# Two seams of a fused attention, gated MLP and expert kernel: splits queued behind the last unit, a check moved, rooms dealt anew

## The chip, the cores and the metric

The kernel runs on one core of a Trainium2 chip. The core has five engines with a queue each: TensorE (PE, matrix products, with its weight loads as PEld), VectorE (DVE), ScalarE (ACT), GpSimd (POOL) and SyncE (SP, which issues most transfers). The metric is the device time of one execution in microseconds. Three executions of the kernel before took 591.48, 587.75 and 591.14 us: the median is 591.14.

## The reference, cut to what matters

Three stages follow one another. B = 2 batches, S = 576 tokens, H = 8 heads of 64, width 512.

```python
# 1. attention in which each row keeps its 32 largest scores
scores = q @ k.T / 8
kth = the 32nd largest score of each row
attn = softmax(where(scores >= kth, scores, -1e9))
x = concatenated heads of attn @ v                        # (2, 576, 512)
# 2. gated MLP that mixes along the tokens
h = gelu(x @ w_in)                                        # 1024 wide
u, v = halves of h
v_n = layernorm(v) * g_ln
v_s = einsum('ts,bsd->btd', w_sg, v_n) + b_sg             # the spatial product
x = x + (u * v_s) @ w_out
# 3. mixture of 8 experts, one per token
logits = x @ w_gate
fresh = argmax(logits)
# a token takes its own choice when it is the first or sigmoid(x @ w_local) < 0.5, else its predecessor's
out = p[e] * (relu(x @ w1[e]) @ w2[e])
```

## The kernel before

**Units.** The attention is cut into tiles of 128 queries and these into units, one head of one tile each: 36 in each batch, 72 in all (`unit`, L348). A unit makes its scores on TensorE (L289), copies them (ScalarE, L292), finds a threshold from maxima (VectorE L318 to L335, ScalarE L329, GpSimd L333), takes exponentials (L331), and masks them: every second unit on VectorE (L345), the others with a sign on ScalarE (L342) and a product on GpSimd (L343). TensorE transposes the result (L357), ScalarE copies it as `pt` (L360), and TensorE multiplies it by the values (L365, `pv`). When four units are through, VectorE divides by the sums and writes the rows (L370 to L382). There is one `pv` buffer, so the next four wait for that.

**Steps between units.** A list `between` holds steps of the later stages, and `pump` (L736) takes some after each unit: the input product of the MLP for a finished tile (`mlp_in`), then, after the last unit, `tail` (L680). `tail` is the spatial product of batch 0 and of batch 1 (`spread`), and `finish`, which works out the logits and the route and projects (`project`, L594) each tile with `w_out`, adds `x` (L610) and writes the rows to `xrows` in device memory (L612). The list `written` keeps these ten writes; the last two belong to the tile that holds the end of both batches.

**Splits.** The products of `spread`, `logits` and `project` work on numbers split in two parts: `in_two` (L453) copies the upper part on ScalarE (L455) and subtracts it on VectorE or GpSimd (L456). `parts` (L480) splits the spatial weights (ScalarE and GpSimd) and the activations of batch 0 (ScalarE and VectorE), five bands each, with one band more of the weights for the second batch; `parts_late` those of batch 1, `parts_out` the projection's weights. The parts lie in rooms of earlier tiles that are no longer in use (`of_scores`, `of_weights`, `of_rest`, `of_queries`, `of_values`).

**The check.** After `attention`, L1081 to L1097 look whether the fast search for the threshold held in every unit, and put a flag in `fi`. The program reads it after the experts; if it is set, everything is done again with an exact search.

**The experts.** `experts` (L817) opens pools of its own in the same memory. VectorE sorts the experts by their counts (L830 on), gives each token a slot (`split`, L854), and a product (`in_slots`, L874) turns slots into token numbers. GpSimd gathers the rows of `xrows` by these numbers, 128 slots at a time (L907); `take` (L934) transposes them into `xw`. SyncE reads the experts' numbers into registers (L1009) and loads the weights (`load_expert`, L952), the first half of the first expert's `w1` behind the last write of `xrows`, the rest behind the second gather. `expert` (L969) makes both products, `give` (L941) writes the result. `KEEP` products without use (L998) stand between the projection and the experts, and `WARM` such products (L802) at the start.

**What sets the order.** Each engine works its queue in order. The orders are made at build time by a planner that simulates the engines with modelled costs: at each step an engine takes, of the instructions that are ready, the one of highest priority. That is its place in the program, moved ahead by `tc.high_priority(offset=...)` (AHEAD for the units, EVAC for the copies out of the accumulators). So an instruction that is ready early may be placed long before its place in the program. `tc.issue_after(ins)` orders what is issued within it behind `ins` on the engine of `ins`, and on no other. A tile whose room is still in use waits for the release.

Of the kernel before, what the change touches and what calls it, by code (L numbers as in the profile page):

```python
# [11 lines left out]
F32 = mybir.dt.float32  # L12
# [15 lines left out]
AHEAD = 2000  # L28
# [9 lines left out]
WARM = 14  # L38
KEEP = 30
# [3 lines left out]
def tile_topk_gmlp_moe(  # L43
# [123 lines left out]
    def attention(fast):  # L167
# [115 lines left out]

        def scores(b, j, i):
# [27 lines left out]
        def weights_fast(s_sb, un):  # L312
# [24 lines left out]
            if MASK[un % len(MASK)] == "a":  # L337
# [5 lines left out]
                nc.gpsimd.tensor_tensor(e_sb, e_sb, mask, op=OP.mult)  # L343
# [4 lines left out]
        def unit(b, j, i, fast):  # L348
# [10 lines left out]
            pt = wk.tile([P, NJ, P], F32, name="pt", bufs=2)  # L359
            nc.scalar.activation(pt.rearrange("p t q -> p (t q)"), pt_ps[:, :NJ * P], AF.Relu)  # L360
# [6 lines left out]
            if i % g == g - 1:  # L367
# [9 lines left out]
                for a in range(w):  # L377
# [3 lines left out]
                    nc.vector.tensor_tensor(xo[to, :, a, :], pv[r, :, a, :D],  # L381
                                            rc[r, :, a, None].to_broadcast([n, g, D]), op=OP.mult)  # L382
# [97 lines left out]
        def parts():  # L480
# [5 lines left out]
            rooms = [of_scores, of_scores] + [of_weights] * 5 + [of_queries] * 3  # L486
# [12 lines left out]
        def parts_late():  # L499

            sg = wts.tile([P, NJ, S], F32, name="w_sg_sb").bitcast(F32R)
            rooms = of_values(F2) + [sg[:, j, :F2] for j in range(NJ)]
# [4 lines left out]
            rooms += [kv.tile([P, S], F32, name="kk", bufs=6).bitcast(F32R)[:, :F2] for _ in range(6)]  # L507
            for f in range(CF):
                UT2[1, f] = (rooms.pop(0), rooms.pop(0))

        def parts_out():
            rooms = [of_weights] * 5 + [of_queries] * 3
            for f in range(CF):
                OUT2.append((rooms.pop(0)(), rooms.pop(0)()))
# [12 lines left out]
        def spread(b):  # L527
# [3 lines left out]
            def step(f, n, j):  # L531
# [3 lines left out]
                if j == js[0] and f == 0 and n == 0:  # L535
                    (parts, parts_late)[b]()
# [603 lines left out]
```

## Time and profile before

| | |
|---|---|
| median of 3 runs | 591.14 us (587.75 to 591.48) |
| the profiled execution | 589.88 us, of which its span 588.1 us |
| TensorE busy | 519.8 us, 88% of the span |
| VectorE, ScalarE, GpSimd busy | 349.1, 307.8, 260.4 us |
| mean granted clock of TensorE | 0.972 |
| transfers | 61.57 MB, mean 105 GB/s |

The span runs from the first to the last instruction of the profiled execution, and all times inside it count from its start. The attention with the input products fills the time to about 345 us, the spatial product and the projection that to about 413 us, the experts the rest. The granted clock is a mean over a stretch: 1.00 is 2.4 GHz, 0.50 is 1.2 GHz. In brackets, a row of a timeline gives the idle time of the engine before it and what ended that.

### The profile page before, as it was taken

The page shows a single profiled execution, that of the slowest core. Times are in us where ns is not written, and L with a number is a line of the kernel's source. Part 1 is how long each engine was busy: PE and PEld are TensorE (multiplying, and loading weights), DVE is VectorE, ACT ScalarE, POOL GpSimd, SP SyncE. Part 2 cuts the span into 40 slices and gives each one's busy share as a digit, 9 for nine tenths or more (in the row PEclk, how much of TensorE's full clock was granted, in tenths as well). Part 3 has the DMA queues.
Part 4 walks back from the last instruction along what each step waited for, and adds up shares of the span by engine and source line. Part 5 has one row for each costly group of instructions (what it writes and reads, how often), then busy time and mean ns, then how long its engine had stood idle before and what let it go on. Part 6 is the DMA issues. An engine that isn't in the chain of part 4 may idle for free. (4 is left out here: it accounts for less than half of the span.)

```text
span 588.1 us, 10456 instructions
## 1 busy us (share of the span) xinstructions
PE 519.8 (88%) x3477; PEld 450.8 (77%) x3478; DVE 349.1 (59%) x1643; ACT 307.8 (52%) x566; POOL 260.4 (44%) x382
## 2 busy tenths in 40 slices
PE   6568698998989898999967899999699999999992
PEld 3447576867778787878857788968399999999992
DVE  4798998989798999999982335764201111111110
ACT  3579879898799989889881614210020111011110
POOL 6497796777667676785855121010220101000010
PEclk9799999999999999999997999999989999999996
DMA  8953210002000002110000000014599997684000
GB/s 175 259 155 111 100 45 6 25 2 75 12 28 20 16 13 82 48 35 17 7 7 20 16 3 1 1 58 150 175 337 386 388 386 269 232 297 162 18 36 17
DMA packets 42610, 61.57 MB, mean 105 GB/s; under 512 B 14056, under 2 KB 18152, under 8 KB 42544
## 3 DMA queue, kind: packets, MB, share of 16 engines
q1 hardware_dynamic: 40880, 55.80, 28.9%
q0 software_dynamic: 1664, 4.97, 2.5%
q8 instruction: 31, 0.51, 0.4%
q14 instruction: 35, 0.29, 0.2%
HBM read 53.68 MB, written 7.33 MB: 104 GB/s over the span
## 5 line engine op out<-in xcount | busy, mean ns | idle before, releaser
L365 PE MATMUL pv<-v,pt 128*128 128x128 f32 (+1 forms) x720 | 101.6, 280 | 8.5 <-DVE row L381 7.1
L333 POOL TENSOR_TENSOR rest<-s_sb,sg 128x576 f32<-128x576 f32 x72 | 93.7, 1302 | 30.5 <-ACT sg L329 29.5
L289 PE MATMUL s_ps<-kk,q 128*128 128x288 f32 x288 | 86.7, 424 | 21.1 <-ACT s_sb L292 20.2
L365 PEld LDWEIGHTS pv<-v,pt 128*128 128x128 f32 x720 | 94.1, 195 | 13.8 <-issue 6.3
L318 DVE MAX8 cand<-s_sb 128x8 f32<-128x72 f32 x576 | 90.0, 222 | 9.2 <-ACT s_sb L292 9.0
L289 PEld LDWEIGHTS s_ps<-kk,q 128*128 128x128 f32 x288 | 50.3, 194 | 37.3 <-ACT s_sb L292 26.8
L357 PE MATMUL pt_ps<-ident,e_sb 128*128 128x128 f32 x360 | 65.1, 281 | 15.5 <-ACT pt L360 8.5
L976 PE MATMUL h_ps<-xw,w_sb 128*128 128x152 f32 (+6 forms) x512 | 78.2, 302 | 0.0
L987 PE MATMUL y_ps<-hT,w_sb 128*128 128x152 f32 (+6 forms) x512 | 75.3, 299 | 0.0
L976 PEld LDWEIGHTS h_ps<-xw,w_sb 128*128 128x128 f32 x512 | 72.9, 192 | 0.4
L987 PEld LDWEIGHTS y_ps<-hT,w_sb 128*128 128x128 f32 x512 | 71.1, 190 | 0.0
L979 ACT ACTIVATE hT<-h_ps 128x152 f32<-128x152 f32 (+6 forms) x32 | 9.7, 302 | 113.9 <-PE h_ps L976 113.1
L357 PEld LDWEIGHTS pt_ps<-ident,e_sb 128*128 128x128 f32 x360 | 44.4, 145 | 27.7 <-issue 6.3
L329 ACT ACTIVATE sg<-s_sb,last 128x576 bf16<-128x576 f32 x72 | 55.6, 772 | 10.8 <-DVE last L321 7.1
L360 ACT ACTIVATE pt<-pt_ps 128x640 f32<-128x640 f32 x72 | 50.3, 698 | 17.0 <-PE pt_ps L357 16.1
L335 DVE MAX8 next<-rest 128x8 f32<-128x583 f32 x72 | 54.8, 761 | 6.4 <-POOL rest L334 6.1
L331 ACT ACTIVATE e_sb<-s_sb,nm 128x576 f32<-128x576 f32 x72 | 55.7, 774 | 4.2 <-POOL nm L326 2.1
L948 POOL DMA_INDIRECT out_dram<-orow,to x10 | 10.0, 1001 | 103.1 <-ACT orow L947 48.3
L292 ACT ACTIVATE s_sb<-s_ps 128x576 f32<-128x576 f32 x72 | 46.4, 644 | 17.0 <-PE s_ps L289 15.1
L343 POOL TENSOR_TENSOR e_sb<-e_sb,mask 128x576 f32<-128x576 f32 x36 | 46.2, 1282 | 16.6 <-ACT mask L342 7.8
L981 DVE TENSOR_SCALAR hT<-h_ps 128x152 f32<-128x152 f32 (+6 forms) x32 | 10.3, 323 | 71.9 <-PE h_ps L976 66.5
L989 DVE COPY yT<-y_ps 128x152 f32<-128x152 f32 (+6 forms) x32 | 9.9, 323 | 64.6 <-PE y_ps L987 64.6
(285 smaller groups left out, 871.7 us busy)
## 6 DMA issues: line engine op xcount, KB each, us to landing
w_sb<-in_w_dram SPq DMA_DIRECT2D x32, 1024.0 KB, 10.5
dbl<-in_w_in_dram SPq DMA_DIRECT2D x8, 512.0 KB, 4.6
kk<-in_kT_dram SPq DMA_DIRECT2D x8, 288.0 KB, 4.2
q<-in_qT_dram SPq DMA_DIRECT2D x32, 64.0 KB, 2.3
v<-in_v_dram SPq DMA_DIRECT2D x8, 256.0 KB, 6.1
dbl<-in_w_out_dram SPq DMA_DIRECT2D x4, 512.0 KB, 3.8
xin<-row SPq DMA_DIRECT2D x8, 256.0 KB, 2.0
back<-xin SPq DMA_DIRECT2D x8, 256.0 KB, 2.8
```

The costliest lines, as they stand in the source:

```text
L289: nc.tensor.matmul(s_ps[:, n, :HS], QH[b, j, h], KK[b, pair][:, n * HS:(n + 1) * HS], start=True, stop=True)
L292: EVACS.append(nc.scalar.activation(s_sb.rearrange("p (n s) -> p n s", n=2), s_ps[:, :, :HS], AF.Copy))
L318: nc.vector.max(cand[:, 8 * g:8 * g + 8], s_sb[:, g * w:(g + 1) * w])
L329: nc.scalar.activation(sg, s_sb, AF.Sign, bias=last8[:, un, 7:8], scale=-LESS, accum_out=cnt)
L331: nc.scalar.activation(e_sb, s_sb, AF.Exp, bias=nm, scale=scale)
L333: nc.gpsimd.tensor_tensor(below[:, :S], s_sb, sg, op=OP.mult)
L335: nc.vector.max(next8[:, un, :], below)
L357: tr = nc.tensor.transpose(pt_ps[:, t * P:(t + 1) * P], p_sb[:, k0:k0 + P], ident)
L360: nc.scalar.activation(pt.rearrange("p t q -> p (t q)"), pt_ps[:, :NJ * P], AF.Relu)
L365: nc.tensor.matmul(PV[b][:, i % g, :], pt[:, t, :], V1[b][:, t, w * i * (D + 1):w * i * (D + 1) + nv], start=t == 0, stop=t == NJ - 1)
L976: nc.tensor.matmul(hp[:, :W], w1_sb[:, c, f * P:(f + 1) * P], xw[:, c, at], start=c == 0, stop=c == CD - 1)
L987: nc.tensor.matmul(yp[:, :W], w2_sb[:, f, c * P:(c + 1) * P], hT[:, f, :W], start=f == 0, stop=f == CE - 1)
```

## The change

It does eight things:

- `WARM` goes from 14 to 7, `KEEP` from 30 to 24; the `KEEP` products are queued behind the first product of the search for slots.
- The last mask product on GpSimd, the last `pt` copy on ScalarE and the last row write on VectorE are noted in `ENDS`, and `parts` and `parts_late` are issued behind them, each engine behind its own.
- The rooms of the split parts change. The parts of the gated `u` go from `w_in` to rooms of the values, `w_sg` and the keys; the batch-1 activations to rooms of the raw loads and of `xT`; the projection's weights to the room of `w_in`.
- `logits` takes its small buffer from `of_rest`.
- In `experts`, `xw` and the gathered rows get pools that are opened ahead of the search's pool `rt`, and `w2` is laid out ahead of `w1`. So the search's tiles lie elsewhere.
- The search has twice the priority offset.
- The first half of the first expert's `w1` is issued behind the fourth last write of `xrows`; the second half stays behind the last.
- The check becomes a function and is called after the second expert.

```diff
-WARM = 14
-KEEP = 30
+WARM = 7
+KEEP = 24
...
+        ENDS = {}
...
-                nc.gpsimd.tensor_tensor(e_sb, e_sb, mask, op=OP.mult)
+                ENDS["g"] = nc.gpsimd.tensor_tensor(e_sb, e_sb, mask, op=OP.mult)
...
-            nc.scalar.activation(pt.rearrange("p t q -> p (t q)"), pt_ps[:, :NJ * P], AF.Relu)
+            ENDS["a"] = nc.scalar.activation(pt.rearrange("p t q -> p (t q)"), pt_ps[:, :NJ * P], AF.Relu)
...
-                    nc.vector.tensor_tensor(xo[to, :, a, :], pv[r, :, a, :D],
+                    ENDS["v"] = nc.vector.tensor_tensor(xo[to, :, a, :], pv[r, :, a, :D],
...
+        def of_transposed():
+            return wk.tile([P, NJ * P], F32, name="pt", bufs=2).bitcast(F32R)[:, :F2]
...
-            rooms = [of_scores, of_scores] + [of_weights] * 5 + [of_queries] * 3
+            rooms = [of_scores, of_scores] + [of_weights] * 5 + [of_transposed, of_transposed, of_queries]
...
-            room = wts.tile([P, 2, CF, F2], F32, name="w_in_sb").bitcast(F32R)
-            for f in range(CF):
-                UT2[0, f] = (room[:, 0, f], room[:, 1, f])
-            UT2[BOTH] = [wk.tile([P, NJ, P], F32, name="pt", bufs=2).bitcast(F32R)[:, :CF] for _ in range(2)]
+            sg = wts.tile([P, NJ, S], F32, name="w_sg_sb").bitcast(F32R)
+            rooms = of_values(F2) + [sg[:, j, :F2] for j in range(NJ)]
+            rooms += [kv.tile([P, S], F32, name="kk", bufs=6).bitcast(F32R)[:, :F2] for _ in range(6)]
+            for b in range(B):
+                for f in range(CF):
+                    UT2[b, f] = (rooms.pop(0), rooms.pop(0))
+            UT2[BOTH] = [of_queries().rearrange("p (c n) -> p c n", n=P) for _ in range(2)]
...
         def parts_late():
-            sg = wts.tile([P, NJ, S], F32, name="w_sg_sb").bitcast(F32R)
-            rooms = of_values(F2) + [sg[:, j, :F2] for j in range(NJ)]
+            rooms = []
+            for _ in range(2):
+                room = raw.tile([P, 2 * DM], U32, name="dbl", bufs=2).bitcast(F32R)
+                rooms += [room[:, :F2], room[:, F2:]]
+            for _ in range(4):
+                room = one.tile([P, CD, P], F32, name="xT", bufs=5).bitcast(F32R)
+                rooms.append(room.rearrange("p c n -> p (c n)"))
...
         def parts_out():
-            rooms = [of_weights] * 5 + [of_queries] * 3
+            room = wts.tile([P, 2, CF, F2], F32, name="w_in_sb").bitcast(F32R)
             for f in range(CF):
-                OUT2.append((rooms.pop(0)(), rooms.pop(0)()))
+                OUT2.append((room[:, 0, f], room[:, 1, f]))
...
-                    (parts, parts_late)[b]()
+                    with ExitStack() as behind:
+                        for ins in ENDS.values():
+                            behind.enter_context(tc.issue_after(ins.ins))
+                        (parts, parts_late)[b]()
...
-            added = raw.tile([P, 2 * DM], U32, name="dbl", bufs=2).bitcast(F32)[:E + 1, :S]
+            added = of_rest()[:E + 1]
...
-    def experts():
+    def experts(check=None):
         own = ExitStack()
         wp = own.enter_context(tc.tile_pool(name="wp", bufs=3))
+        inp = own.enter_context(tc.tile_pool(name="inp", bufs=1))
+        rows = own.enter_context(tc.tile_pool(name="rows", bufs=1))
         rt = own.enter_context(tc.tile_pool(name="rt", bufs=1))
...
-        ahead.enter_context(tc.high_priority(offset=AHEAD))
+        ahead.enter_context(tc.high_priority(offset=2 * AHEAD))
...
-        xw = slots.tile([P, CD, NC * P], F32, name="xw")
+        xw = inp.tile([P, CD, NC * P], F32, name="xw")
...
-            xr = moe.tile([P, DM], F32, name="xr", bufs=4)
+            xr = rows.tile([P, DM], F32, name="xr", bufs=4)
...
+            w2_sb = wp.tile([P, CE, DM], F32, name="w2_sb")
             w1_sb = wp.tile([P, CD, FE], F32, name="w1_sb")
-            w2_sb = wp.tile([P, CE, DM], F32, name="w2_sb")
...
-                with tc.issue_after(written[-1]) if after is not None else ExitStack():
+                with tc.issue_after(written[-1 if g else -4]) if after is not None else ExitStack():
...
-        for m in range(KEEP):
-            nc.tensor.matmul(idle, ones, place[0][:, :4, :], start=m == 0, stop=m == KEEP - 1)
+        with tc.issue_after(found[0].ins):
+            for m in range(KEEP):
+                nc.tensor.matmul(idle, ones, place[0][:, :4, :], start=m == 0, stop=m == KEEP - 1)
...
             expert(w, slice(OFF[r], end_r), partial(take_up_to, OFF[r + 1] + WIDTHS[r + 1] if r + 1 < E else 0))
+            if r == 1 and check is not None:
+                check(ps_a)
...
-    fa = const.tile([P, UNITS], F32, name="fa")
-    nc.vector.tensor_scalar(fa, next8[:, :, 7], 1e-30, None, op0=OP.is_le)
...
-    fi = const.tile([P, 1], I32, name="fi")
-    with tc.tile_pool(name="ps_r", bufs=1, space=PSUM) as ps_r:
-        fp = ps_r.tile([P, 1], F32, name="fp")
+    fi = const.tile([P, 1], I32, name="fi")
+
+    def check(ps_a):
+        fa = const.tile([P, UNITS], F32, name="fa")
+        nc.vector.tensor_scalar(fa, next8[:, :, 7], 1e-30, None, op0=OP.is_le)
...
+        fp = ps_a.tile([P, 1], F32, name="a_ps")
         nc.tensor.matmul(fp, ones, fs, start=True, stop=True)
         nc.vector.tensor_copy(fi, fp)
-    experts()
+
+    experts(check)
```

## Rows read from the trace of the kernel before

**Rows 1.** Busy time by stretch: stretch, its length, engines' busy (count), clock, DMA.
```profile
300.00:320.00 20.00, 12.46 (x89) 11.97 (x90) 12.79 (x18) 9.26 (x14) 14.31 (x12) 0.83 0.04 15
...
314.00:316.00 2.00, 2.00 (x12) 2.00 (x11) 0.00 (x0) 1.10 (x2) 0.59 (x1) 0.50 0.00 0
...
400.00:410.00 10.00, 10.00 (x45) 8.18 (x44) 3.82 (x20) 0.00 (x0) 0.00 (x0) 1.00 0.51 158
...
420.00:430.00 10.00, 5.40 (x23) 3.61 (x22) 0.00 (x0) 1.79 (x3) 7.01 (x16) 0.77 0.78 248
430.00:440.00 10.00, 10.00 (x50) 9.71 (x49) 1.18 (x3) 1.31 (x3) 1.23 (x2) 0.89 1.02 366
```

**Rows 2.** TensorE's timeline, 305 to 346 us: start, length, instruction, count, idle before.
```profile
305.85 0.74 PE L357 MATMUL pt_ps<-ident,e_sb 128*128 128x128 f32 x5 [1.49 <-ACT pt L360]
311.97 2.47 PE L365 MATMUL pv<-v,pt 128*128 128x128 f32 x10 [5.39 <-DVE row L381]
...
337.93 3.84 PE L418 MATMUL m_ps<-xT,w_in_sb 128*128 128x128 f32 x32 [0.69 <-ACT xT L404]
...
345.89 0.40 PE L523 MATMUL m_ps<-v,s_sb 128*128 128x288 f32 x1
```

**Rows 3.** VectorE's timeline, 303 to 312 us.
```profile
303.33 3.78 DVE L1082 TENSOR_SCALAR fa<-next 128x72 f32<-128x72 f32 x1
...
308.61 1.35 DVE L1089 TENSOR_SCALAR fc<-fc 128x72 int32<-128x72 int32 x1
...
310.00 1.23 DVE L1090 TENSOR_TENSOR fa<-fa,fc 128x72 f32<-128x72 f32 x1
...
311.41 0.41 DVE L381 TENSOR_TENSOR row<-pv,rc 128x256 f32<-128x256 f32 x1
```

**Rows 4.** GpSimd's timeline, 308 to 312 us.
```profile
308.52 1.40 POOL L456 TENSOR_TENSOR s_sb<-w_sg_sb,v 128x576 fp32r<-128x576 f32 x1 [1.48 <-DVE e_sb L345]
309.87 1.27 POOL L343 TENSOR_TENSOR e_sb<-e_sb,mask 128x576 f32<-128x576 f32 x1
```

**Rows 5.** VectorE's timeline: the counts' copy and the search's first instruction.
```profile
396.69 0.24 DVE L677 COPY pos<-pt_ps 128x88 f32<-128x88 f32 x1
...
408.26 0.17 DVE L830 SCALAR_TENSOR_TENSOR key<-pos,iota_e 128x8 f32<-128x8 f32 x1
```

**Rows 6.** SyncE: the last row writes (timeline), and L1009 (min/median/max ns, first and last).
```profile
417.15 1.11 SPq L612 DMA_DIRECT2D xrows<-back  x2
...
L1009 SPq TENSOR_LOAD <-regs_i x8: 263/272/539, 411.7 to 416.5; - x8
```

**Rows 7.** GpSimd's timeline, 420 to 423 us.
```profile
420.50 0.36 POOL L993 MEMSET yT<- 128x4 f32 x9 [35.58 <-DMA xrows<-back]
421.52 1.24 POOL L907 DMA_INDIRECT xr<-xrows,frm  x1 [0.66 <-issue]
```

**Rows 8.** TensorE's timeline, 414 to 452 us.
```profile
414.27 4.48 PE L998 MATMUL y_ps<-slot_at_l,ones 128*128 128x512 bf16 x19 [1.25 <-DVE back L610]
...
425.20 0.88 PE L938 MATMUL a_ps<-ident,xr 128*128 128x128 f32 x4 [3.80 <-issue]
...
428.85 7.91 PE L976 MATMUL h_ps<-xw,w_sb 128*128 128x224 f32 x32
...
444.22 8.11 PE L987 MATMUL y_ps<-hT,w_sb 128*128 128x224 f32 x42
```

**Rows 9.** The last unit's copy (ScalarE's timeline), and splits by line (L455, L456).
```profile
333.46 0.70 ACT L360 ACTIVATE pt<-pt_ps 128x640 f32<-128x640 f32 x1 [1.20 <-PE pt_ps L357]
...
L455 ACT ACTIVATE v<-w_sg_sb x5: 669/670/670, 185.0 to 187.3; 128x576 fp32r<-128x576 f32 x5
...
L456 DVE TENSOR_TENSOR e_sb<-vn,e_sb x2: 692/692/693, 327.4 to 331.6; 128x512 fp32r<-128x512 f32 x2
```

**Rows 10.** The start: the useless products, and VectorE's first weights (timelines).
```profile
2.57 4.66 PE L802 MATMUL m_ps<-tri,ones 128*128 128x512 bf16 x14 [2.57 <-POOL none L134]
...
18.13 0.69 DVE L197 TENSOR_SCALAR m_ps<-dbl 128x512 uint32<-128x512 uint32 x1 [3.50 <-DMA dbl<-in_w_in_dram]
```

More of the change, by code (lines that the diff above doesn't have):

```diff
@@ L358, in unit @@
             BACK.append(tr)
-            pt = wk.tile([P, NJ, P], F32, name="pt", bufs=2)
-            nc.scalar.activation(pt.rearrange("p t q -> p (t q)"), pt_ps[:, :NJ * P], AF.Relu)
+            pt = wk.tile([P, NJ * P], F32, name="pt", bufs=2).rearrange("p (t q) -> p t q", t=NJ)
+            ENDS["a"] = nc.scalar.activation(pt.rearrange("p t q -> p (t q)"), pt_ps[:, :NJ * P], AF.Relu)
             g, w, nv = (4, 1, NV) if j < NJ - 1 else (2, 2, 2 * (D + 1))
@@ L380, in unit @@
                     n = LAST if w > 1 else P
-                    nc.vector.tensor_tensor(xo[to, :, a, :], pv[r, :, a, :D],
-                                            rc[r, :, a, None].to_broadcast([n, g, D]), op=OP.mult)
+                    ENDS["v"] = nc.vector.tensor_tensor(xo[to, :, a, :], pv[r, :, a, :D],
+                                                        rc[r, :, a, None].to_broadcast([n, g, D]), op=OP.mult)
         BOTH = (B, NJ - 1)
@@ L506, in parts_late, with parts_out @@
                     in_two(VN2[1, j], vn_of(1, j), nc.gpsimd)
-            rooms += [kv.tile([P, S], F32, name="kk", bufs=6).bitcast(F32R)[:, :F2] for _ in range(6)]
+        def parts_out():
+            room = wts.tile([P, 2, CF, F2], F32, name="w_in_sb").bitcast(F32R)
             for f in range(CF):
-                UT2[1, f] = (rooms.pop(0), rooms.pop(0))
-        def parts_out():
-            rooms = [of_weights] * 5 + [of_queries] * 3
-            for f in range(CF):
-                OUT2.append((rooms.pop(0)(), rooms.pop(0)()))
+                OUT2.append((room[:, 0, f], room[:, 1, f]))
                 in_two(OUT2[f], w_out_sb[:, f], nc.gpsimd)
@@ L872, in experts @@
         place = split(sl, 0, NC, "slot")
+        found = []
         def in_slots(place, parts, name):
@@ L881, in in_slots @@
             for t in range(NT):
-                nc.tensor.matmul(ps, at_low[:, t, :], at[:, t], start=t == 0, stop=t == NT - 1)
+                mm = nc.tensor.matmul(ps, at_low[:, t, :], at[:, t], start=t == 0, stop=t == NT - 1)
+            found.append(mm)
             got = rt.tile([P, n], F32, name=name)
@@ L1067, in experts @@
                 nc.vector.tensor_copy(pq, pslot2[:, ds(q, 1)])
-                xr = moe.tile([P, DM], F32, name="xr", bufs=4)
+                xr = rows.tile([P, DM], F32, name="xr", bufs=4)
                 nc.gpsimd.indirect_dma_start(out=xr, out_offset=None, in_=xrows,
@@ L1079, in tile_topk_gmlp_moe @@
     attention(True)
[L1081 to L1095 removed]
+    fi = const.tile([P, 1], I32, name="fi")
+    def check(ps_a):
+        fa = const.tile([P, UNITS], F32, name="fa")
+        nc.vector.tensor_scalar(fa, next8[:, :, 7], 1e-30, None, op0=OP.is_le)
+        nc.vector.scalar_tensor_tensor(fa, last8[:, :, 7], 0.0, fa, op0=OP.is_le, op1=OP.max)
+        fc = const.tile([P, UNITS], I32, name="fc")
+        nc.vector.tensor_scalar(fc, cnts, float(2 * TOP - 2 - S), None, op0=OP.add)
+        nc.vector.scalar_tensor_tensor(fa, fc, float(2 * ADD), fa, op0=OP.is_gt, op1=OP.max)
+        nc.vector.scalar_tensor_tensor(fa, fc, 0.0, fa, op0=OP.is_lt, op1=OP.max)
+        nc.vector.tensor_scalar(fc, fc, 1, None, op0=OP.bitwise_and)
+        nc.vector.tensor_tensor(fa, fa, fc, op=OP.max)
+        fs = const.tile([P, 1], BF16, name="fs")
+        nc.vector.tensor_reduce(fs, fa, axis=AX.X, op=OP.max)
+        fp = ps_a.tile([P, 1], F32, name="a_ps")
         nc.tensor.matmul(fp, ones, fs, start=True, stop=True)
         nc.vector.tensor_copy(fi, fp)
[L1098 removed]
+    experts(check)
     redo = nc.values_load(fi[0:1, 0:1], min_val=0, max_val=P)
```

9 lines of the change are left out of this document (removed).

## The prediction

> **What bounds the kernel now.** I read the busy shares by stretch first, because the mean hides where TensorE rests. From 340 us to 413 us and from about 430 us to 577 us it is busy without a break at full clock; there only fewer products would help, and the change takes none away [rows 1]. What is left are two seams. The first is 300 to 320 us, where the last units of the top-k attention run out: 12.5 us busy of 20, clock 0.83. The second is 420 to 430 us, between the projection and the experts: 5.4 us busy of 10, clock 0.77, and 0.89 in the ten after [rows 1].
>
> The timeline of TensorE shows what the first seam waits for. It rests 5.39 us before the pv products at 311.97, released by the VectorE line that writes the attention rows (L381); those ten products then take 2.47 us, at a clock that had fallen meanwhile. After the last unit the input product of the last tile runs from 337.93, and the first spatial product begins at 345.89 [rows 2]. VectorE's own timeline says why L381 was late. From 303.33 to 312 it mostly does the check of the search, which nobody needs before the end: L1082 lasts 3.78 us for 72 numbers a partition, L1089 1.35, L1090 1.23, and L381, needed by TensorE, comes last at 311.41 [rows 3]. These lengths are not arithmetic. L1089 and L1090 end within 0.1 us of the GpSimd operation beside them (308.52 and 1.40; 309.87 and 1.27), and L1082 is about as long as three of those. GpSimd meanwhile does splits of the spatial weights (L456, 1.40 us each), one of which waits 1.48 us for VectorE, and only then the mask product of a unit (L343) at 309.87 [rows 3, 4]. So two kinds of work that could wait, the check and the splits, stand in the last units' queues and hold one another up.
>
> In the second seam the searching of slots begins with L830 at 408.26, although its input is ready some 11 us earlier (the counts are copied at 396.69) [rows 5]; the last row is added just ahead of 414.27 [rows 8]. On SyncE the writes of the last rows go out at 417.15 only, because eight register loads (L1009) stand before them from 411.7 to 416.5 [rows 6]. GpSimd then waits until 420.50 for those rows to land, clears yT, and starts the first gather at 421.52 [rows 7]. TensorE meanwhile runs the useless products, rests 3.80 us, and begins the experts at half clock: 32 products in 7.91 us [rows 8].
>
> **The change, part by part.**
>
> Splits behind the last unit. The bound on the gain is what TensorE loses here: 5.39 us of rest at 311.97, 1.49 us at 305.85, and the half clock until about 316. The clock is still at its lower level (0.50, that is 1.2 GHz) at 314 to 316, so TensorE works at half speed from 311.97 to 316 at least: some 2.1 us lost [rows 1, 2]. Together 9.0 us. The least: the check's instructions have nothing that ties them to their new place, so the planner may put them again between the last units. Then L1082 and its like wait for one mask product of GpSimd at a time (1.27 us), no longer for several operations in a row; three such waits are 3.8 us against the 6.4 us that L1082, L1089 and L1090 take now, and 2.6 us are won [rows 3, 4]. I take 6.5, nearer the upper end, since the split ahead of L343 goes for certain, and it alone, with its wait of 1.48 us, puts that product back by 2.9 us.
>
> What this part adds. The eleven copies on ScalarE at 0.67 us start only when the last unit's pt is out at 334.16: 7.4 us and the copy of xT, to 342 [rows 9]. Five of them had been done at 185 us, beside the attention, where ScalarE had room. GpSimd's six subtractions of 1.40 follow from about 335.5 to 343.9. VectorE's five at 0.69 [rows 9] finish by 340 if the two engines run freely, and by 347.3 if VectorE gets in only behind GpSimd. TensorE wants the first pair at 345.89 and the fifth some 1.6 us later [rows 2]: so the cost lies between nothing and 2.1 us, hidden by the input product of the last tile (from 337.93). I take 0.5, because VectorE's operations get in where GpSimd waits for a copy.
>
> On this the Trainium skill (SBUF — State Buffer, section "SBUF: two separate sides") speaks against the change: a VectorE operation with two SBUF inputs and a reading GpSimd operation exclude each other for their whole length. By it the two engines' splits add up instead of overlapping, and the sum would take the 2.1. The trace agrees in L1089 and L1090 [rows 3, 4]; it has no stretch with both kinds of split side by side.
>
> Rooms dealt anew. The parts of u, the projection's weights and the split activations change places; none of these is late now, TensorE being full from 345 to 413, so I cost it at nothing; its cover is that full engine. What matters is that the search's tiles no longer lie where the spatial product's operands are read until 408. The search then falls beside the projection, and the register loads too. The last write may go out right after the last row is added, at 414.3 instead of 417.15: 2.9 us. If yT is cleared earlier, another 1.0 us between 420.50 and 421.52 goes [rows 5 to 7]. Against it: half of the first expert's weights, 1 MB, now goes out ahead of the last rows' writes; at the 366 GB/s of 430 to 440 us that is 2.9 us of transfers which the rows may have to wait for [rows 1]. So 0 to 3.9; I take 3.4, since the megabyte goes out while TensorE still works on the last two tiles, and most of it can land by then.
>
> Useless products ahead of the experts: 24 instead of 30, and no longer ahead of the search's own. They cost nothing while the rows are under way. At 0.236 us (19 in 4.48) they last 5.7 us, from 414.27 to 419.9, and the first expert's rows would be there at 425.20 - 3.4 = 421.8: a rest of 1.9 instead of 3.80 us [rows 8]. If the clock holds, the 32 products of 7.91 us take 1.7 us less (0.193 us each once it is full, from the 42 behind them [rows 8]). I take half, 0.8; 0 to 1.7.
>
> Useless products at the start: 7 for 14. Fourteen take 4.66 us from 2.57, so the first scores could start some 1.5 us earlier. But VectorE then stands 3.50 us for the first weights at 18.13, and that load's time does not hang on TensorE [rows 10]. So nothing; at best 1.4, at worst nothing either, as the same 3.5 us also hide a slower start.
>
> Check behind the second expert: nine small VectorE operations and one product of a column, beside products that keep TensorE full; nothing. Its old place is costed above. The first write to the output and the tail stay.
>
> **Sum**: 6.5 - 0.5 + 3.4 + 0.8 = 10.2 us off the profiled execution's 589.88, so 579.7. That execution lies 1.3 under the median of the runs (591.14).
>
> **Rivals.**
>
> *The check comes back and the splits are paid.* VectorE's check stays between the last units (2.6 instead of 6.5), and the spatial product waits the whole 2.1 us. For it: nothing but its place in the program holds the check, and it was put there by the same freedom before. Then 2.6 - 2.1 + 3.4 + 0.8 = 4.7: 585.2.
>
> *The second seam does not move.* The rows land as late as now because the weights' megabyte goes first, or because yT's clearing still stands ahead of the gathers. For it: the cost of 2.9 us above is as large as the gain. Then 6.0 alone: 583.9.
>
> *Slower: the attention is planned worse.* Seven products fewer shift the planner's clock at the start by 1.5 us, and with new rooms the orders of all queues are dealt again. The 72 units (two batches of 36, by the code) take about 300 us, 4.2 us each; if that pace grows by 0.25 us, 18 us are lost, and 589.88 - 10.2 + 18 = 597.7. It decides from 0.22 us a unit on, where the sum comes out 1% above the time before. Against it: in the units TensorE, ScalarE and VectorE are all near full, and nothing in the units' own code changes.
>
> By the Trainium skill (TensorE: Matmul & The Clock Gate, section "What's actually happening") the clock starts throttled and only activity releases it, so seven leading products could leave the first scores slow. In the trace the quicker spacing starts with the eighth product; the 3.5 us at 18.13 would hide it, and the sum stays.
>
> **How the numbers follow.** Forecast (two seams shorter, 573 to 583): 0.62. Check and splits: 0.15. Second seam unmoved: 0.16. Slower: 0.07. Of the two middle cases more than half stays under 585.2, which is 1% below the median; a measurement here cannot tell less than that 1% from no change. So faster 0.80, same 0.13, slower 0.07. The best case of all bounds is 9.0 + 3.9 + 1.7 + 1.4 = 16.0, or 573.9; the worst without a slower plan is 2.6 - 2.1 = 0.5, or 589.4. The range from 573.5 to 587 takes in the first and most of the second.
>
> **What would show it.** In the first seam: no rest over 2 us between 300 and 320, the clock at 1.00 there, GpSimd without a split before the last L343, and the first spatial product near 339 instead of 345.89. If the check's lines still stand before L381, the first rival is at work; if TensorE rests before that product, its second half. In the second: L830 near the copied counts, L1009's loads before the last rows are added, the first gather some 10 us before its old time. The forecast is wrong if the last unit ends where it did, if the pace of the units changes, or if TensorE shows new rests in the spatial product, where a room is not yet free.

## The result, and the profile after

The changed kernel takes 596.31 us (median of 4 runs, 595.7 to 597.27) against 590.02 for the one before on the same chip (4 runs): ratio 1.0112, interval 1.0071 to 1.0152. It is slower by 1.1%, where 579.7 was forecast with a range up to 587. The profiled execution took 596.42 us, its span 594.7.

Both gains that the forecast was built on are there in part, and each was paid for elsewhere. The table gives the times at which the same events fall in the two traces.

| event (us from the start of the span) | before | after | later by |
|---|---|---|---|
| pt of the last unit ends | 334.2 | 335.6 | 1.4 |
| last xT copy ends | 337.9 | 342.2 | 4.3 |
| first spatial product | 345.9 | 352.35 | 6.5 |
| last row added | 414.2 | 420.5 | 6.3 |
| first gather | 421.5 | 428.5 | 7.0 |
| first product of the experts | 428.85 | 435.99 | 7.1 |

A second measure is used below: how far a kernel is *behind*, that is, how much later its TensorE has finished the same amount of useful work (each matmul weighed by its usual spacing) than TensorE of the kernel before. By it the changed kernel is 4.1 us ahead at 72 us and 1.9 ahead at 187, then 2.8 behind at 211 and 10.2 behind at 298; at 329 only 0.9; at 352 again 6.5, and 7.0 at the end. So it loses 12 us in the second half of the attention, wins 9.3 in its last units, and loses 5.6 right behind them. Other weights for the products move these figures by some tenths of a us.

Busy time by stretch of the changed kernel, the columns as in [rows 1]:

```profile
300.00:320.00 20.00, 17.27 (x141) 15.86 (x140) 13.75 (x56) 17.28 (x27) 10.75 (x13) 1.00 0.06 21
...
340.00:350.00 10.00, 7.72 (x37) 6.73 (x38) 7.65 (x5) 3.79 (x8) 10.00 (x7) 0.66 0.01 2
400.00:410.00 10.00, 10.00 (x54) 8.00 (x53) 8.80 (x43) 0.00 (x0) 0.00 (x0) 1.00 0.43 150
420.00:430.00 10.00, 5.34 (x24) 2.25 (x23) 0.53 (x1) 0.00 (x0) 1.24 (x1) 0.93 0.43 134
430.00:440.00 10.00, 7.12 (x26) 6.09 (x27) 0.39 (x1) 1.79 (x3) 6.08 (x15) 0.56 0.79 240
```

Against [rows 1], 300 to 320 is now well filled (17.3 us of TensorE for 12.5, clock 1.00 for 0.83), in part with work that the kernel before had behind it by then. A new hole stands at 340 to 350, where TensorE was full before, and the second seam, 7 us later now, is no fuller than it was. TensorE's timeline shows the two holes (compare [rows 2, 8]):

```profile
2.56 3.05 PE L815 MATMUL m_ps<-tri,ones 128*128 128x512 bf16 x7 [2.56 <-POOL none L134]
...
314.94 1.35 PE L367 MATMUL pv<-v,pt 128*128 128x128 f32 x10 [0.32 <-DVE row L383]
...
342.28 5.94 PE L420 MATMUL m_ps<-xT,w_in_sb 128*128 128x128 f32 x32 [3.89 <-ACT xT L406]
...
352.35 0.40 PE L533 MATMUL m_ps<-v,s_sb 128*128 128x288 f32 x1
...
420.58 5.34 PE L1019 MATMUL y_ps<-slot_at_l,ones 128*128 128x512 bf16 x24 [0.78 <-DVE back L623]
432.13 1.12 PE L958 MATMUL a_ps<-ident,xr 128*128 128x128 f32 x4 [6.20 <-DMA xr<-xrows,frm]
...
435.99 7.65 PE L996 MATMUL h_ps<-xw,w_sb 128*128 128x224 f32 x32
```

The wait of 5.39 us for the attention rows has shrunk to 0.32. But the last tile's input product waits 3.89 us for the copy of xT, against 0.69 before, and then takes 5.94 us for 3.84, because the clock fell during the rest (0.66 over the ten us). ScalarE's timeline names what stood ahead of that copy:

```profile
334.89 0.70 ACT L362 ACTIVATE pt<-pt_ps 128x640 f32<-128x640 f32 x1 [1.20 <-PE pt_ps L359]
335.49 1.14 ACT L457 ACTIVATE dbl<-vn 128x512 fp32r<-128x512 f32 x2
...
338.14 2.39 ACT L457 ACTIVATE v<-w_sg_sb 128x576 fp32r<-128x576 f32 x4
...
341.65 0.58 ACT L406 ACTIVATE xT<-m_ps 128x512 f32<-128x512 f32 x1
```

From 335.49 to 341.65 ScalarE does twelve copies for the splits without a break, among them the five of w_sg that were done at 185 us before [rows 9], and only then the one that TensorE waits for. VectorE's and GpSimd's timelines, in this order, show the splits beside one another and the two ends of the search:

```profile
310.90 0.40 DVE L1112 TENSOR_SCALAR fc<-cnts 128x72 int32<-128x72 f32 x1 [0.99 <-ACT sg L331]
...
314.71 1.15 DVE L1109 SCALAR_TENSOR_TENSOR fa<-last,fa 128x72 f32<-128x72 f32 x1
...
339.17 1.88 DVE L458 TENSOR_TENSOR e_sb<-vn,e_sb 128x512 fp32r<-128x512 f32 x1
...
402.99 0.17 DVE L847 SCALAR_TENSOR_TENSOR key<-pos,iota_e 128x8 f32<-128x8 f32 x1
```

```profile
336.19 2.51 POOL L458 TENSOR_TENSOR dbl<-vn,dbl 128x512 fp32r<-128x512 f32 x2 [6.93 <-ACT dbl L457]
338.66 8.65 POOL L458 TENSOR_TENSOR s_sb<-w_sg_sb,v 128x576 fp32r<-128x576 f32 x5
...
428.52 1.24 POOL L927 DMA_INDIRECT xr<-xrows,frm  x1 [67.92 <-issue]
```

The check came back among the last units (310.90, 314.71), but in short pieces: with no split on GpSimd beside it, nothing holds it up as in [rows 3, 4]. The search starts at 402.99, 5.3 us earlier than in [rows 5]. Its gain is lost on SyncE (compare [rows 6]):

```profile
416.33 1.75 SPq L625 DMA_DIRECT2D xrows<-back  x2
420.02 0.41 SPq L979 DMA_DIRECT2D w_sb<-in_w_dram  x1
420.56 1.31 SPq L625 DMA_DIRECT2D xrows<-back  x2
```

The first half of w1, 1 MB (L979), now stands ahead of the last two row writes. Its room becomes free only with the last projection product (L533), so SyncE waits 1.7 us for that, until 419.83, and the rows go out behind the megabyte. The wait itself costs little: the last row is added at 420.53, and the two writes are issued at 420.56 and 421.4, sooner after it than before (2.9 us, [rows 6, 8]). What is lost is lost on the way. The summary of transfers from 405 to 432 us (count, size, median us from issue to landing) has those two writes as:

```profile
xrows<-back SPq DMA_DIRECT2D x2, 128.0 KB, 6.2
```

Before, the same row of the same stretch reads 2.4: 3.8 us are lost there, against the 2.9 that the earlier issue wins. The first gather starts 8.0 us after the last row is added; before it was 7.3 [rows 7].

### The profile page after: what moved, and what is told of

It is laid out like the page before. It is cut to its first block, busy times and chain, and to the rows that moved or that the text cites. A ratio compares the mean times of both kernels' runs of the same rounds, so it can differ in the third digit from the quotient of the medians.

```text
span 594.7 us, 10424 instructions
## 1 busy us (share of the span) xinstructions
PE 523.3 (88%) x3465; PEld 454.7 (76%) x3465; DVE 349.5 (59%) x1643; ACT 307.4 (52%) x566; POOL 262.9 (44%) x382
## 5 line engine op out<-in xcount | busy, mean ns | idle before, releaser
L367 PE MATMUL pv<-v,pt 128*128 128x128 f32 (+1 forms) x720 | 103.2, 280 | 12.2 <-DVE row L383 7.1
L291 PE MATMUL s_ps<-kk,q 128*128 128x288 f32 x288 | 91.0, 442 | 16.8 <-ACT s_sb L294 15.7
L320 DVE MAX8 cand<-s_sb 128x8 f32<-128x72 f32 x576 | 88.6, 217 | 13.6 <-ACT s_sb L294 13.4
L291 PEld LDWEIGHTS s_ps<-kk,q 128*128 128x128 f32 x288 | 52.5, 202 | 35.4 <-ACT s_sb L294 23.4
L359 PE MATMUL pt_ps<-ident,e_sb 128*128 128x128 f32 x360 | 67.2, 283 | 13.2 <-ACT pt L362 9.9
L359 PEld LDWEIGHTS pt_ps<-ident,e_sb 128*128 128x128 f32 x360 | 46.4, 148 | 22.1 <-ACT pt L362 9.0
L337 DVE MAX8 next<-rest 128x8 f32<-128x583 f32 x72 | 54.6, 758 | 11.1 <-POOL rest L336 10.5
L362 ACT ACTIVATE pt<-pt_ps 128x640 f32<-128x640 f32 x72 | 50.2, 697 | 17.3 <-PE pt_ps L359 14.9
L1001 DVE TENSOR_SCALAR hT<-h_ps 128x152 f32<-128x152 f32 (+6 forms) x32 | 10.3, 323 | 78.2 <-PE h_ps L996 78.2
L927 POOL DMA_INDIRECT xr<-xrows,frm x10 | 9.9, 989 | 102.1 <-issue 68.8
L294 ACT ACTIVATE s_sb<-s_ps 128x576 f32<-128x576 f32 x72 | 46.2, 642 | 15.5 <-PE s_ps L291 15.3
```

The lines of the kernel that those rows point to most:

```text
L291: nc.tensor.matmul(s_ps[:, n, :HS], QH[b, j, h], KK[b, pair][:, n * HS:(n + 1) * HS], start=True, stop=True)
L320: nc.vector.max(cand[:, 8 * g:8 * g + 8], s_sb[:, g * w:(g + 1) * w])
L337: nc.vector.max(next8[:, un, :], below)
L359: tr = nc.tensor.transpose(pt_ps[:, t * P:(t + 1) * P], p_sb[:, k0:k0 + P], ident)
L362: ENDS["a"] = nc.scalar.activation(pt.rearrange("p t q -> p (t q)"), pt_ps[:, :NJ * P], AF.Relu)
L367: nc.tensor.matmul(PV[b][:, i % g, :], pt[:, t, :], V1[b][:, t, w * i * (D + 1):w * i * (D + 1) + nv], start=t == 0, stop=t == NJ - 1)
```

## The experiments

How far each kernel is behind the one before at six points of its work (named by the time at which the kernel before is there), with its time. Negative is ahead.

| kernel | 72 | 211 | 298 | 329 | 352 | end | median us | ratio, interval |
|---|---|---|---|---|---|---|---|---|
| changed | -4.1 | +2.8 | +10.2 | +0.9 | +6.5 | +7.0 | 596.31 | 1.0112 (1.0071 to 1.0152) |
| 1: changed, 14 lead | +0.7 | +4.5 | +13.9 | +4.9 | +10.1 | +10.3 | 600.25 | 1.0155 (1.0121 to 1.0188) |
| 2: changed, splits not held | -3.0 | -0.4 | +6.9 | +1.3 | +1.1 | +2.3 | 591.99 | 1.0032 (1.0005 to 1.006) |
| 3: before, 7 lead | -2.6 | +0.4 | +7.9 | +2.4 | +4.1 | +7.4 | 594.75 | 1.0065 (1.0038 to 1.0092) |
| 4: before, splits held | +1.2 | +5.1 | +15.4 | +6.5 | +11.9 | +12.1 | 600.9 | 1.0166 (1.0129 to 1.0202) |
| 5: before, subtractions held | +1.0 | +0.9 | +0.6 | -6.7 | -5.4 | -5.4 | 583.9 | 0.9889 (0.9867 to 0.9911) |
| 6: changed, xT first | -3.5 | +2.8 | +10.4 | +1.1 | +3.6 | +6.6 | 597.78 | 1.013 (1.0111 to 1.015) |
| 7: changed, megabyte last | +0.3 | +6.5 | +14.1 | +4.8 | +9.9 | +7.0 | 593.62 | 1.0046 (1.0022 to 1.0071) |
| 8: changed, subtractions held | -3.1 | +0.1 | +5.5 | -0.5 | +0.6 | +1.3 | 588.67 | 0.9976 (0.9958 to 0.9994) |
| 9: three details put otherwise | +0.5 | +0.5 | +0.6 | -6.8 | -6.6 | -9.6 | 579.97 | 0.9818 (0.98 to 0.9835) |
| 10: before, five copies held | +0.6 | +4.4 | +13.5 | +5.1 | +9.9 | +10.3 | 601.1 | 1.0185 (1.015 to 1.022) |
| 11: before, 12 lead | +0.9 | +1.3 | +7.7 | +2.1 | +2.1 | +2.6 | 594.42 | 1.0073 (1.0053 to 1.0092) |
| 12: before, 18 lead | +1.1 | 0.0 | +8.2 | +2.7 | +4.3 | +4.3 | 593.27 | 1.0043 (1.0025 to 1.0061) |

The columns are each kernel's one profiled execution, the times the medians of its runs; single executions of the kernels that don't lead with 14 lie up to 7 us apart. The runs were made on several chips, so the ratios, each to the kernel before on the same chip, compare better than the medians.

**Which part re-deals the attention (1 to 4).** The attention was 10 us late before it came to any place that the forecast had costed. By the traces only two parts of the change touch the attention at all: the number of leading products, from some 13 us on, and the holding back of the splits, from 185 us on. Rooms, experts and check alter nothing before the attention's end: kernels 1 and 4, which differ in these and in what comes behind the attention, run the same lines in the same order on TensorE, VectorE, ScalarE and GpSimd until 345 us, behind the last unit, and so do 2 and 3 until 331. So each of the two was put back alone, and done alone.

```
1:  WARM = 14                      (changed kernel)
2:  (parts, parts_late)[b]()       (changed kernel, without issue_after over ENDS)
3:  WARM = 7                       (kernel before)
4:  ENDS and its issue_after       (kernel before)
```

> The changed kernel with 14 useless products at the start instead of 7, nothing else. Theory A (the start's 7 products re-deal the planner's order of the whole attention, and that costs the 14 us by which TensorE falls back between 72 and 300 us, from 4 us ahead of the kernel before to 10 us behind): the fall goes, TensorE is within 3 us of the kernel before at 295 us, and the time is 596.3 less about 8 to 10, so 586 to 589. Theory B (splits taken out of the attention re-deal it): the fall stays, 595 to 598.

> The changed kernel without the splits' queueing behind the last unit; rooms, check, search and 7 leading products as changed. Theory A: the fall of the attention stays (10 us behind at 295 us); the last units' stalls come back (7 to 9 us), and the copy of xT is not behind the splits any more (5 us back): 598 to 602. Theory B: the fall goes: 588 to 593.

> The kernel before with 7 useless products at the start. Theory A: TensorE falls back in the attention as in the changed kernel, and the time is 8 to 12 above the kernel before: 598 to 602. Theory B: within 2 us of the kernel before, 588 to 592.

> The kernel before with the splits queued behind the last unit, nothing else. Theory A: no fall in the attention; the last units win 7 to 9 us, the copy of xT behind eleven split copies on ScalarE loses 5 with the half clock after it: 585 to 589. Theory B: the attention falls back by some 10 us: 594 to 598. In both, the last copy of xT ends over 6 us after the last copy of pt, against 3.7 in the kernel before.

Theory A fell as the one cause: with 14 products the changed kernel is no faster (600.25), and 7 on the kernel before cost 4.3 us, between what the two theories had said. Theory B holds, more strongly than expected: holding the splits back costs 10.5 us on the kernel before, and without it the changed kernel is 4.3 us faster. Kernel 4 shows both losses of the changed one: 15.4 behind at 298 us, and 5.4 more between 329 and 352.

**Copies or subtractions (5, 8, 10).** A split is a copy on ScalarE and a subtraction on GpSimd or VectorE. The rule holds both back. In 5 (on the kernel before) and 8 (on the changed one) only the subtractions are held; in 10 only the five copies of w_sg are held, with the subtractions that need them.

```
 def in_two(parts, full, eng, late=False):
     nc.scalar.activation(hi, full, AF.Copy)
-    return eng.tensor_tensor(lo, ...)
+    with issue_after(each of ENDS) if late:    (5, 8: here; 10: around the copy, for w_sg alone)
+        return eng.tensor_tensor(lo, ...)
```

> The kernel before, with one part of the change cut smaller: only the subtractions of the splits (GpSimd, VectorE) wait in the planner's order for the last unit; ScalarE's copies for them stay free, so that the five copies of w_sg at 185 us stay where they were and the planned order of TensorE is the one of before up to about 266 us. Theory C (the loss comes from holding back ScalarE's copies: that re-deals the attention from 185 us on, and puts xT's last copy behind twelve copies): the last units gain their 6 to 9 us and nothing is lost before or behind them: 581 to 587. Theory D (the held subtractions themselves cost as much as they save, because GpSimd's eleven at 1.4 to 1.9 us each now stand between the last unit and the spatial products): 592 to 600, as for the whole rule on the kernel before (600.9).

> The changed kernel, with ScalarE's copies for the splits free again and only the subtractions waiting for the last unit. The five copies of w_sg are taken in at about 185 us as in the kernel before, though the attention's order is another than before (7 products lead). Theory C: xT's copy no longer stands behind the copies (-5) and the attention is dealt as in the kernel of before with 7 products, which was 7.9 behind at 298 us instead of 10.2: 586 to 591. Theory D: 594 to 598.

> The kernel before, with only the five copies of w_sg for the splits (ScalarE, 185.0 to 187.3 us in the trace of before) held in the planned order behind the last unit; their subtractions come behind them, all other copies and subtractions are free as before. Theory G (taking these five out of the gap at 185 us re-deals the rest of the attention, and that is what costs 10 to 15 us by 298 us): scores of the last unit at 302 us or later, 5 us lost by 211 us and 10 or more by 298 us; the last units then win back their 7: 592 to 600. Theory H (the attention's loss comes from the other held copies and subtractions): at 298 us within 3 us of before, 582 to 589.

Kernel 5 is the clean test of the gain: all four engines run in the order of before up to about 257 us, TensorE even up to 313, it is 0.6 behind at 298 and 6.7 ahead at 329, so the last units won 7.3. The check was still in its old place there. Its timelines of TensorE, GpSimd and ScalarE, in this order:

```profile
307.29 1.35 PE L367 MATMUL pv<-v,pt 128*128 128x128 f32 x10 [0.51 <-DVE row L383]
...
332.49 3.84 PE L420 MATMUL m_ps<-xT,w_in_sb 128*128 128x128 f32 x32 [1.40 <-ACT xT L406]
```

```profile
321.56 4.31 POOL L461 TENSOR_TENSOR s_sb<-w_sg_sb,v 128x576 fp32r<-128x576 f32 x3
...
331.70 3.66 POOL L461 TENSOR_TENSOR s_sb<-w_sg_sb,v 128x576 fp32r<-128x576 f32 x2
```

```profile
331.34 0.61 ACT L457 ACTIVATE e_sb<-vn 128x512 fp32r<-128x512 f32 x1
331.86 0.57 ACT L406 ACTIVATE xT<-m_ps 128x512 f32<-128x512 f32 x1
```

The copies being done early, GpSimd can subtract from 321.56 on, while the last units run without it, and only four copies stand ahead of xT's. Theory C holds, D fell. Kernel 8 says the same from the other side: 7.6 us faster than the changed kernel.

Kernel 10 is Theory G's case: five copies of 0.67 us, moved, cost 10 us or more. Its busy time by stretch and, under it, that of the kernel before in the same two stretches:

```profile
195.00:200.00 5.00, 0.74 (x5) 0.53 (x5) 3.08 (x8) 4.97 (x8) 3.41 (x4) 1.00 0.00 0
200.00:205.00 5.00, 4.78 (x23) 4.34 (x24) 3.00 (x16) 0.80 (x2) 0.66 (x3) 0.66 0.00 0
```

```profile
195.00:200.00 5.00, 4.43 (x26) 3.34 (x27) 4.92 (x30) 4.97 (x8) 3.99 (x7) 1.00 0.10 26
200.00:205.00 5.00, 4.21 (x30) 3.38 (x29) 4.78 (x27) 4.77 (x11) 2.86 (x6) 1.00 0.00 2
```

TensorE all but stops from 195 to 200 us (0.74 busy of 5) and comes back at a lower clock (0.66). VectorE's timeline of kernel 10 shows why:

```profile
196.87 0.77 DVE L337 MAX8 next<-rest 128x8 f32<-128x583 f32 x1 [1.93 <-POOL rest L336]
...
197.75 1.61 DVE L444 TENSOR_SCALAR vn<-row,mv,rs 128x512 f32<-128x512 f32 x1
...
199.57 0.59 DVE L383 TENSOR_TENSOR row<-pv,rc 64x128 f32<-64x128 f32 x2
```

Without the five copies the planner lines the units up otherwise. L383, which TensorE needs for its next pv products, now stands behind L337, which waits 1.93 us for GpSimd, and behind L444; it runs at 199.57. In the kernel before, the same instruction ran at 196.76 and TensorE waited 0.38. More such places must follow by 298 us (13.5 behind); only this one was traced through. Kernel 4 runs in the same order as kernel 10 on all engines up to about 258 us, so what it has lost by then it has lost by these five copies.

**The first seam (6).** In the changed kernel, the split work is queued behind the last copy of xT as well:

```
-            nc.scalar.activation(XT[t], ps, AF.Copy)
+            ENDS["x"] = nc.scalar.activation(XT[t], ps, AF.Copy)
```

> The changed kernel, with the split work queued behind the last copy of xT as well, not behind the last unit alone. The attention is planned as in the changed kernel. Theory C: the last xT copy ends at about 338 to 339 instead of 342.2, the last projection runs 3 to 4 us earlier and the spatial product starts at 347 to 349 instead of 352.4: 591 to 593.5. Theory D: GpSimd's subtractions end last anyway and the copies for them now start later: 595 to 599.

Its TensorE timeline:

```profile
339.22 3.84 PE L420 MATMUL m_ps<-xT,w_in_sb 128*128 128x128 f32 x32 [0.69 <-ACT xT L406]
...
347.18 0.40 PE L533 MATMUL m_ps<-v,s_sb 128*128 128x288 f32 x1
...
355.40 0.40 PE L533 MATMUL m_ps<-v,s_sb 128*128 128x288 f32 x1 [1.56 <-DVE ut L563]
...
362.82 0.40 PE L533 MATMUL m_ps<-v,s_sb 128*128 128x288 f32 x1 [0.77 <-DVE ut L568]
```

The spatial product starts at 347.18 as Theory C had it, 5.2 us earlier than in the changed kernel, and then gives nearly all of it back (1.3 behind at 342 us, 5.9 at 373): GpSimd's subtractions of w_sg now run from 343.92 to 352.66, and VectorE's work beside them is slow as well. The total is no better (597.78; Theory D). So the first seam was closed twice, by xT's place and by the pile of subtractions behind it, and only earlier copies (5, 8) open both.

**The second seam (7).** Both halves of w1 behind the last row write, as in the kernel before:

```
-  with tc.issue_after(written[-1 if g else -4]) if after is not None ...
+  with tc.issue_after(written[-1]) if after is not None ...
```

> The changed kernel, with both halves of the first expert's w1 behind the last row write, as it was for both before. Theory E (SyncE's wait for the room of the first half holds the last two row writes back, and the megabyte then shares the queues with them): row writes land 3 to 5 us earlier after the last row added, first gather earlier by as much, 592 to 594. Its rival F (the first half then comes late for the first expert's product, and the search is in place anyway): first gather earlier, but the first expert's products wait for w1: 595 to 598.

Its TensorE timeline at the start and at this seam:

```profile
8.49 2.29 PE L291 MATMUL s_ps<-kk,q 128*128 128x288 f32 x4 [0.74 <-ACT s_sb L294]
...
424.00 5.34 PE L1019 MATMUL y_ps<-slot_at_l,ones 128*128 128x512 bf16 x23 [0.78 <-DVE back L623]
432.39 1.11 PE L958 MATMUL a_ps<-ident,xr 128*128 128x128 f32 x4 [3.06 <-DMA xr<-xrows,frm]
...
436.27 3.98 PE L996 MATMUL h_ps<-xw,w_sb 128*128 128x224 f32 x14
```

and its two last row writes in the summary of transfers:

```profile
xrows<-back SPq DMA_DIRECT2D x2, 128.0 KB, 3.2
```

From the last row added (423.9) to the first product of the experts it needs 12.3 us; the changed kernel needed 15.5, the kernel before 14.6. TensorE rests 3.06 us for 6.20. Theory E holds, and no wait for w1 shows (F). The other kernels bear it out: the same distance is 14.7 to 15.9 us in the five with the megabyte first (the changed one, 1, 2, 6, 8), and 11.8 in the other one that has it last (9). Its profiled execution ran some 4 us later than the changed kernel's from the start on, for a reason of its own (last section), so its row of the table carries those 4 us all along; the medians differ by 2.7 us.

**The number of leading products (11, 12, with 3).** The kernel before with `WARM = 12` and `WARM = 18`.

> The kernel before with 12 products in front of the attention instead of 14. All that they do to the work after them is to plan it from another moment on. Theory I (the planner's order is a draw: any other number of leading products gives another order of the attention, some us better or worse by 298 us): -4 to +8 at 298 us, and a total that differs from before by more than 1.5 us, with neither sign excluded: 586 to 597. Theory J (7 products cost their 4.3 us because fewer of them are worse, in proportion): 591 to 592.

> The kernel before with 18 products in front of the attention. Theory I (a draw, as for 12): differs from before by more than 1.5 us either way, 586 to 597. Theory J (fewer are worse, more better or the same): 588 to 590.5.

Theory J fell: more are no better than fewer. With 7, 12 and 18 the kernel before is 7.9, 7.7 and 8.2 us behind at 298, and 4.3, 4.4 and 3.2 us slower in the medians. Theory I fits: another number gives another order. That all three come out worse says that the order with 14 was a lucky or a chosen one; four numbers don't tell how rare it is.

**The three details together (9).** The changed kernel with 14 leading products, only the subtractions held, and both halves of w1 last.

> The changed kernel with three of its details put otherwise: 14 leading products as before, only the subtractions of the splits held behind the last unit (ScalarE's copies free), and both halves of the first expert's w1 behind the last row write. TensorE's planned order is that of before up to about 266 us. If the three losses found so far are all that ate the gains: -7 at the last units and +1 to 2 at the first seam, as where the subtractions alone were held on the kernel before (583.9), and -2 to -3 at the second seam, where the changed kernel with the megabyte last needed 12.4 us from the last row added to the first expert's product against 14.6 before: 580 to 582.5. If the gain at the second seam came of that run's own order and not of the early search: 583 to 586.

It takes 579.97 us, 1.8% less than the kernel before, and 16 less than the changed one. It keeps the order of before up to about 257 us, wins 7.4 in the last units, loses 0.2 where the changed kernel lost 5.6, and wins 3.0 at the second seam: 11.8 us there (407.5 to 419.31). Its GpSimd timeline, two rows of TensorE's, and its busy time behind the seam:

```profile
411.73 1.24 POOL L927 DMA_INDIRECT xr<-xrows,frm  x1 [64.15 <-issue]
...
416.71 0.39 POOL L1013 MEMSET yT<- 128x4 f32 x9
```

```profile
415.52 1.11 PE L958 MATMUL a_ps<-ident,xr 128*128 128x128 f32 x4 [2.60 <-DMA xr<-xrows,frm]
...
419.31 6.18 PE L996 MATMUL h_ps<-xw,w_sb 128*128 128x224 f32 x24
```

```profile
417.00:427.00 10.00, 9.60 (x43) 8.84 (x44) 0.78 (x2) 2.55 (x5) 3.75 (x8) 0.74 0.95 325
```

The gather starts 4.2 us after the last row is added, and the clearing of yT no longer stands ahead of it. What the new rooms, the twofold priority and the fewer useless products each have in this was not tried apart. That the time is the forecast 579.7 almost to the digit is in part luck: the first seam gave more than forecast (7.4 for 6.5), the second less (3.0 for 3.4 and 0.8 together).

## Why the prediction was wrong, step by step

*The seams.* Both were read rightly: 7.3 us lay in the last units (kernel 5) and 2.9 in the second seam (kernel 9, 11.8 for 14.6 us). Ahead of the forecast's steps, though, stood the order of the attention, which it took as given. Of the 16.6 us between forecast and result, letting the splits' copies go gives back 7.6 (kernel 8), and 14 leading products with the megabyte last another 8.7 (from 8 to 9); the megabyte alone gave 2.7 (kernel 7).

*Splits behind the last unit, 6.5 (2.6 to 9.0).* Right: 7.3 where nothing else moved. That the check's instructions would come back was right too, and cheap as argued: the wait for one mask product at a time. The check's own move was not run alone; in kernel 5 it stays in its old place, and the stall is gone all the same.

*"What this part adds", 0.5 (0 to 2.1): the step that failed most.* What failed is the price of moving the splits' copies: 0.5 us in the sum, 17 on the kernel before (kernel 4 for 5, medians) and 7.6 in the changed one (against kernel 8). The prediction wrote that five copies "had been done at 185 us, beside the attention, where ScalarE had room", that all eleven now run to 342 "and the copy of xT", and then costed only what the first spatial product waits for. Two prices were left out. First, what the copy of xT makes wait: the input product of the last tile, 3.89 us of rest and 2.1 more at a lower clock, which was named as the cover of this cost and was itself what came late. Second, what filled ScalarE's room at 185 us when the five were gone: another order of the units. Between kernels 4 and 5, which differ in the held copies (and a clearing of 0.57 us on GpSimd held with them), lie 14.8 us at 298, 13.2 at 329 and 17.5 at the end. In the changed kernel the attention runs in yet another order, so the price is another, too. The bound of 2.1 doesn't follow from its rows, either: by them the last split is there at 347.3, and the fifth pair is wanted at about 347.5.

*Splits side by side.* VectorE's five and GpSimd's six were put at 0 to 2.1 together. In the changed kernel VectorE's subtractions take 1.43 to 1.95 us beside GpSimd's, against 0.68 for one of the kind alone in kernel 5 (at 338.74), and GpSimd's five of w_sg 1.73 each for 1.40 [rows 4]. By the Trainium skill (SBUF — State Buffer, section "SBUF: two separate sides") a VectorE operation with two SBUF inputs and a GpSimd operation that reads exclude each other; the trace comes near that, since waiting out one whole GpSimd subtraction would make 2.08 (1.40 and 0.68). (Of the two instructions of the check that the prediction set beside the rule, only L1090 has two inputs; L1089 has one.) No rest shows in the changed kernel only since its product starts 6.5 us late; kernel 6, where it starts early, rests 1.56 and 0.77 us and loses 4.6.

*Second seam, 3.4 (0 to 3.9): the wrong end.* Search and register loads came forward as argued. The price of the megabyte was seen (2.9 us), and set aside with "the megabyte goes out while TensorE still works on the last two tiles". It could not: its room is read by the projection to the end. So it goes out at 420.02, just ahead of the last two writes, and they land after 6.2 us for 2.4. This is the second rival's mechanism, and it went below its "unmoved": 0.9 us lost instead of 2.9 won.

*The clock, 0.8.* Failed with the step above, and by itself: in the changed kernel TensorE rests 6.20 us, the clock is 0.56 from 430 to 440, and the 32 products take 7.65 us for 7.91 [rows 8]. But in kernel 9, too, where it rests only 2.60 us, the clock is 0.74 from 417 to 427, and the first 24 products take 6.18 us, 0.26 each, as slow as before (0.25).

*Seven leading products, nothing.* Wrong: the start is 1.3 us earlier at 18 us and 4.1 at 72, and it re-deals the attention. On the kernel before 7 cost 4.3 us, in the changed kernel they seem to save 2.5 (by the ratios, whose intervals overlap) to 3.9 (by the medians; kernel 1): a draw, not a price.

*Rooms and check, nothing.* Right as far as seen: between 352 and 405 us the changed kernel falls no further behind (6.5, then 6.1).

*The slower rival.* "The attention is planned worse" had a chance of 0.07 and 597.7 us; the time came out at 596.3. Its mechanism was half right: the orders were dealt again, by the held copies above all, and the new rooms it named had no part. What spoke against it ("nothing in the units' own code changes") was no argument: an order that a planner writes across all queues changes with what is put between the units.

## What to carry to other kernels

Where a planner orders the queues, an instruction that is taken out of a gap changes what comes after it, too: price a moved instruction at both places, and hold a change to the queue whose wait it is to end (here the subtractions, not the copies that feed them). When work is queued behind an event, list what else is waiting on that engine for the same event, and put the item of the longest chain first. A large transfer just ahead of small writes makes these land late (here 6.2 us for 2.4), and one that has to wait for its room may come to stand just there; so it belongs behind the small writes that something waits for.

## What the runs showed of the hardware

With seven leading products the first scores did not always run at the quicker pace. The first four score products take 1.13 us in the changed kernel's trace and in all seven with 12 or more leading products run after it; with 7 they take 1.56 and 1.59 us in kernels 3 and 8 and 2.12 to 2.25 in 2, 6 and 7. In kernel 7 the products stay at half the pace until past 20 us (2.29 us for four, as in its row at 8.49, against 1.24), which made that execution 3 us late at 18 us, and it stayed so. The granted clock reads 1.00 in these stretches all the same (in kernel 7 from 0 to 30 us), so at the start the spacing of the products is what tells, and at which level the clock was the profile does not show. The Trainium skill (TensorE: Matmul & The Clock Gate, section "What's actually happening") has the clock start throttled, and the slow stretch at the start differ between runs of one kernel; the pace in these rows agrees, though it is shown across kernels, one execution each, and the granted clock does not show it. The prediction had held that a wait of VectorE for the first weights (3.50 us [rows 10]) would hide it: in kernel 7 it did not, the scores being later than the weights.
